# Weight loads issued in another place of GpSimd's queue, and another bias in the order of the last part

## The chip, the cores and the metric

The kernel runs on one core of one Trainium2 chip. The metric is the device time of an execution in microseconds, here the median of nine runs. A profile comes from one further execution; its times have their zero at the first instruction of the span.

## The reference

Two layers. The first is attention with a soft cap over 8 batches, 12 heads, 448 tokens and heads of 64: `softmax(cap * tanh(q k^T / 8 / cap)) v` with `cap = 30`. Its result, `x` of shape (8, 448, 768), goes into the second, a mixture of four attention experts with causal masks:

```
logits = x @ w_gate                      # 4 experts, the best 2 are kept per token
w = softmax over the 2 kept logits
for e in range(4):
    q, k, v = x @ wq[e], x @ wk[e], x @ wv[e]          # 768 -> 64 each
    a = softmax(causal(q k^T / 8))
    out += mask_e * w_e * (a @ v @ wo[e])              # 64 -> 768
```

## The kernel before

**Units of work.** The first layer goes by pairs of heads: 48 pairs, six for a batch. For each pair q, k and v are loaded in f32, cast to f16 (`a_cast`, on GpSimd from pair 2 on), q and k are transposed on TensorE (`a_tr`), the scores come in four fills of PSUM (`fill`, L470 to L484), ScalarE takes the tanh of each fill (L510) and then one exponential over the whole pair (L516). The product with v (`a_pv`, L544 and L550) is divided by the row sums and transposed into `xT`, the input of the second layer. Two PSUM buffers hold score fills, so that a fill waits for the tanh of the fill two before it.

When the six pairs of a batch stand in `xT`, the second layer of that batch is planned (`batch`, L1120): projections q and k for two groups of heads, `r` 0 and 1 (L724), values and gate logits in one product with `wvg` (L640; this tile holds the value weights of all four experts and the gate's), the scores and their exponential (L781), the product with the values (L808), and the output projections `wops` (L863) with their evacuation into `ob` and a store.

**Order.** The order of ScalarE's work is written out as a list `prog`: slot p (`("S", p)`), then the tanhs of pair p with the exponential of pair p - 1 and those of the second layer (`"X"`) between them. What TensorE and VectorE do between the fills is chosen while the program is built, by `Plan`: it keeps modelled times of the engines and, in `plan.done`, of each result, has a list of work with costs and due times, and always takes from what can start first the item with the earliest due time. A load of weights is such a result too: key `("w", ("q", r))`, `("w", ("k", r))`, `("w", "v")` or `("w", "o")`, with a time that is set when it is issued. Those times are read when `batch(0)` puts the projections of batch 0 on the list at slot 6. They change the order in which TensorE gets its instructions, not what an instruction waits for on the chip.

**Slots.** `slot(p)` (L1046) issues the loads of later pairs on SyncE, casts pair p + 4 on GpSimd, and issues weight loads on GpSimd's queue. GpSimd does its instructions in order, so that a weight load behind a cast leaves when the cast has had its data. There are 16 weight loads in the list `loads` (L961): q and k of expert 0, q and k of expert 1, four of `wvg`, q and k of experts 2 and 3, four of the output weights. Before the change each of the slots 0 to 7 issues two, behind its cast (L1064 to L1068), and gives them the time `plan.act + 26`, where `plan.act` is ScalarE's modelled time.

**The last part.** When the list is through, what is left of batch 6 and the second half of batch 7 (`last_batch`, L1250) is put into a `Graph` with costs, engines and PSUM banks. `solve` draws 4000 orders: each is built as a list schedule that takes, among what can start within a short time of the first, the operation of highest priority; priorities are the length of the longest path to the end plus a bias, changed at random by up to 3 us for some operations, and the order with the shortest modelled end is kept. The biases are set in L1273. BW is subtracted for the output projections and the stores of batch 6 (`c` in the code), so that -5 puts them forward by 5 us:

```
elif key[0] in ("wo", "st"):
    bias = BA * (key[1] == b and key[2] < 2) - BW * (key[1] == c)
```

Of the kernel before, what the change touches and what calls it, by code (L numbers as in the profile page):

```python
# [239 lines left out]
def kernel(  # L240
# [13 lines left out]
    nc = tc.nc  # L254
# [39 lines left out]
    def load(p, n=2):  # L294

        b, j = divmod(p, HP)
        h0, h1 = 2 * j, 2 * (j + n)
        qf = stage.tile([QP, 2 * n, QC * Dh], f32, name=f"qf_{p}", tag="qf")
        kf = stage.tile([128, 2 * n, KC * Dh], f32, name=f"kf_{p}", tag="kf")
        vf = stage.tile([128, 2 * n, KC * Dh], f32, name=f"vf_{p}", tag="vf")  # L300
        ktf = stage.tile([128, n, Dh], f32, name=f"ktf_{p}", tag="ktf")
        vtf = stage.tile([128, n, Dh], f32, name=f"vtf_{p}", tag="vtf")
        for i in range(n):
            h = slice(2 * i, 2 * i + 2)
            staged[p + i] = (qf[:, h], kf[:, h], vf[:, h], ktf[:, i], vtf[:, i])

        def rows(dst, src, c):
            return lambda eng: eng.dma_start(dst, src.rearrange("h (p c) d -> p h (c d)", c=c))

        def tails(dst, src, i):  # L310
            t = src[b, h0:h1, KM:S].rearrange("(j two) p d -> two p j d", two=2)
            return lambda eng: eng.dma_start(dst[64 * i : 64 * (i + 1)], t[i])

        return [
            rows(qf, q[b, h0:h1], QC), rows(kf, k[b, h0:h1, 0:KM], KC), tails(ktf, k, 0),
            tails(ktf, k, 1), rows(vf, v[b, h0:h1, 0:KM], KC), tails(vtf, v, 0), tails(vtf, v, 1),
        ]
# [6 lines left out]
    def ahead(p, n, since, more=4):  # L324

        new = range(p + n + more * (p > since), p + n + more * (p >= since) + 1)
        return [i for i in new if i < NP]
# [48 lines left out]
    def a_cast(p):  # L376
        if p >= NP:
            return
        eng = nc.vector if p < 2 else nc.gpsimd
        assert p < 8 or ("tr", p - 8) in plan.done  # L380
        assert p < 12 or ("pv", p - 12, 1) in plan.done
        qf, kf, vf, ktf, vtf = staged.pop(p)
        q16 = hd.tile([QP, QC, 2, Dh], f16, name=f"q16_{p}", tag="q16", bufs=8)
        k16 = hd.tile([128, KC, 2, Dh], f16, name=f"k16_{p}", tag="k16", bufs=8)
        eng.tensor_copy(q16, qf.rearrange("p h (c d) -> p c h d", c=QC))  # L385
        nc.gpsimd.tensor_copy(  # L386
            k16, kf.rearrange("p h (c d) -> p c h d", c=KC)
        )
        for g in range(2):
            r = slice(64 * g, 64 * (g + 1))  # L390
            eng.tensor_copy(ktz[p % 8][r, r], ktf[r, :])  # L391
        cast[p] = (q16, k16)
        vcast[p] = (vf, vtf)
        if p > 1:
            a_castv(p)
# [506 lines left out]
    plan = Plan()  # L902
# [35 lines left out]
    def b_const(i):  # L938
        if i == 0:
            nc.gpsimd.memset(ltm, 0.0)  # L940
            nc.gpsimd.affine_select(
                out=ltm, in_=ltm, compare_op=ALU.is_ge, fill=-60000.0, base=0,
                pattern=[[1, 128]], channel_multiplier=-1,
            )
        else:
            nc.vector.memset(vtL, 0.0)
            nc.vector.memset(vtL[64:128, :, Dh : Dh + 1], 1.0)
        nc.vector.memset(vtB[i], 0.0)
        nc.vector.memset(vtB[i][0:64, 0:E:2, Dh : Dh + 1], 1.0)
        nc.vector.memset(vtB[i][64:128, 1:E:2, Dh : Dh + 1], 1.0)  # L950
        for t in pB[2 * i : 2 * i + 2]:
            nc.vector.memset(t[:, 0:64], 0.0)
# [8 lines left out]
    loads = []  # L961
# [81 lines left out]
    for p in range(len(UNITS), NP + HP + 4):  # L1043
        nom.setdefault(("S", p), t)

    def slot(p):  # L1046

        plan.work[:] = [u for u in plan.work if u["key"][0] != "warm"]
        n = 9 if p < 3 else 6 if p < 7 else 3 if p < 13 else 0
        for i in range(n):  # L1050
            plan.done["from", p, i] = nom["S", p] + 7.0 + 5.6 * i / n
            plan.add(("warm", p, i), 0.22, 0.0, [("from", p, i)], 1.0e9, keep_warm)
        if p % 2 == 0:
            for i in ahead(p, LOAD, DEEP):
                if i % 2 == 0:
                    for f in load(i):
                        f(nc.sync)
        for i in ahead(p, CAST, DEEP + 2):
            a_cast(i)
            plan.done[("cast", i)] = max(  # L1060
                5.65 * i + 1.5 if i < 12 else 0.0,
                plan.act + 4.0 + 3.5 * (i - p - CAST) * (p == DEEP + 2),
            )
        for _ in range(2):  # L1064
            if loads:
                w, dst, src = loads.pop(0)
                nc.gpsimd.dma_start(dst, src)
                plan.done["w", w] = plan.act + 26.0  # L1068
        if p in (4, 5):
            b_const(p - 4)  # L1070
        for i in (1, 2) if p == 0 else ahead(p, TR, DEEP + 4, 4):
            plan.add(("tr", i), 0.43, 0.95, [("cast", i)], nom["S", i] - 3.0, a_tr, i)
        if 1 <= p < len(UNITS):
            u = UNITS[p - 1]
            es = [("E", u)]
            due = nom["S", p + 1] + 2.0
            if isinstance(u, tuple):
                i = "AB".index(u[1])
                u = u[0]
                plan.parts(("pv", u, i), 2, 0.47, 0.55, es, due, a_pv, u, i)  # L1080
                d = [("pv", u, i)]
                plan.add(("xt", u, "AB"[i]), 0.12, 0.27, d, due, a_xt_part, u, i)
            else:
                plan.parts(("pv", u, 0), 2, 0.47, 0.55, es, due, a_pv, u, 0)
                d = [("pv", u, 0)]
                plan.parts(("pv", u, 1), 2, 0.47, 0.55, d, due, a_pv, u, 1)
                plan.add(("xt", u), 0.22, 0.35, [("pv", u, 1)], due, a_xt, u)
        if p >= HP and p % HP == 0 and p < NP:
            batch(p // HP - 1)
        if p == NP - 1:  # L1090
            last_qk()
        if p == NP:
            last_vg()
# [6 lines left out]
    def last_qk():  # L1100
        for r in range(2):
            g = ("qk", "A", r)
            due = nom["X", B - 1, r, 0] - 2.0
            for j in range(NDC):
                d = [x_of(j, "A"), ("w", ("q", r)), ("w", ("k", r))] + [(*g, j - 1)] * (j > 0)
                plan.add(
                    (*g, j), 0.22, 0.66 * (j == NDC - 1), d, due, qk_mm, "A", r, j,
                    aux={0: "open", NDC - 1: "close"}.get(j), group=g,
                )
# [10 lines left out]
    def batch(b):  # L1120
        x = ("xt", HP * b + HP - 1)
        t0, t1 = nom["X", b, 0, 0], nom["X", b, 1, 0]
        for r, t in enumerate((t0, t1)):
            plan.parts(("q", b, r), 3, 1.13, 0.55, [x, ("w", ("q", r))], t - 4.0, b_qk, b, r, "q")
            plan.parts(("k", b, r), 3, 1.13, 0.55, [x, ("w", ("k", r))], t - 4.0, b_qk, b, r, "k")
        for n in range(4):
            d = [("v", b, n - 1)] if n else [x, ("w", "v")]
            plan.parts(("v", b, n), 2, 0.66, 0.6, d, t0 + 2.0 * n, b_v, b, n)
        plan.add(("g1", b), 0.0, 1.0, [("v", b, 3)], t1 + 1.0, b_gate, b, aux=None)
        plan.add(("g", b), 0.0, 0.8, [("g1", b), ("G", b)], t1 + 3.0, b_gate2, b, aux=None)  # L1130
        for e in range(E):
            due = t1 + 6.0 + 3.0 * e
            d = [("X", b, e // 2, 1), ("g", b)] + [("pvB", b, e - 1)] * (e % 2)
            plan.add(("pvB", b, e), 0.31, 0.7, d, due, b_pv, b, e)
            if e % 2:
                plan.add(("oT", b, e // 2), 0.22, 0.35, [("pvB", b, e)], due, b_ot, b, e // 2)
        for n in range(4):
            for f in range(2):
                i = 2 * n + f
                d = [("oT", b, 1), ("w", "o")] if i == 0 else [("wo", b, *divmod(i - 1, 2))]  # L1140
                due = t1 + 19.0 + 1.5 * i
                plan.add(("wo", b, n, f), 0.33, 0.5, d, due, b_wo, b, n, f)
# [107 lines left out]
    def last_batch():  # L1250


        p, b = NP - 1, B - 1
# [16 lines left out]
            dict(aux=[(0.0, t) for t in plan.aux], tail=[(0.0, t3)] * 4),  # L1270
        )

        BR, BA, BW, BX = 0.0, 0.0, -5.0, 0.0  # L1273

        BOTH = ("aux", "tail")

# [124 lines left out]
        n = S - CUT  # L1401
# [75 lines left out]
        done = {}  # L1477
# [126 lines left out]
    for pos, o in enumerate(prog, 1):  # L1604
# [22 lines left out]
        while nfill < len(reads) and nfill - 2 in ends and all(  # L1627
            plan.known(d) for d in fill_dep(reads[nfill])
        ):
            do_fill()  # L1630
    last_batch()
# [1 line left out]
_INS = ['q', 'k', 'v', 'cap', 'moe_w_gate', 'moe_wq', 'moe_wk', 'moe_wv', 'moe_wo']  # L1633
# [31 lines left out]
```

## Time and profile before

| | us |
|---|---|
| median of 9 runs | 324.34 |
| lowest and highest | 322.97, 327.56 |
| profiled execution, its own time | 322.86 |
| its span, first to last instruction | 321.1 |
| ScalarE busy | 306.5 |
| TensorE busy (matmul) | 284.9 |
| GpSimd busy | 157.0 |
| share of the 16 DMA engines: SyncE's queue, GpSimd's queue | 52.0%, 6.8% |

In the rows of slices each digit is a fortieth of the span, 8 us, in tenths of busy time. A row of a timeline has start, length, engine, line and operation, the result and its inputs, and in brackets the idle time ahead of it and what ended that. A row of waits has who waited for what, the sum, the number and the longest. The chain is the work that ended last, followed back from the end.

### The profile page before, as it was taken

Reading aid. Unit: us, or ns where it says so; the run is one execution under the profiler, and the core shown is the slowest. Engines: PE = TensorE matmul, PEld = TensorE weight load, DVE = VectorE, ACT = ScalarE, POOL = GpSimd, SP = SyncE. Lnnn points to the kernel's source line nnn. Section 1 sums busy time; section 2 is a strip of 40 time slices with the busy share of each in tenths; the row PEclk is TensorE's granted clock in tenths of the full one; section 3 lists DMA queues with packets and bytes.
Section 4 is the critical chain, followed back from the end, with each engine's and each line's share of the span. In section 5 each row is a group of like instructions: output and inputs, shape, how many; then the busy total and the mean of one; then the engine's idle time right before and its main releaser. Section 6 shows DMA issues by size and latency. Waiting matters only on the chain.

```text
span 321.1 us, 9088 instructions
## 1 busy us (share of the span) xinstructions
PE 284.9 (89%) x3439; PEld 179.5 (56%) x3439; DVE 216.2 (67%) x760; ACT 306.5 (95%) x311; POOL 157.0 (49%) x480
## 2 busy tenths in 40 slices
PE   8887878997999889997799899997999878999993
PEld 2454444664565656565556565655655654557761
DVE  4444544587586877678867876767856975578673
ACT  3999997999999999999999999999999999999973
POOL 4639999956706299874904386082905200220200
PEclk9999999999999999999999979999899999999998
DMA  8679999998025999577082934586012102020045
GB/s 166 176 190 257 226 227 230 241 228 160 1 100 145 254 259 268 160 203 170 2 224 110 281 80 143 161 229 157 3 52 98 27 2 99 2 77 2 3 171 174
DMA packets 65404, 46.22 MB, mean 144 GB/s; under 512 B 26000, under 2 KB 61968, under 8 KB 65360
## 3 DMA queue, kind: packets, MB, share of 16 engines
q1 hardware_dynamic: 54064, 43.28, 52.0%
q0 software_dynamic: 10512, 1.58, 6.8%
q10 hardware_dynamic: 784, 0.77, 0.9%
q8 instruction: 27, 0.44, 0.6%
q14 instruction: 17, 0.14, 0.1%
HBM read 36.19 MB, written 11.01 MB: 147 GB/s over the span
## 4 chain that ended last, share of the span: by engine, by line
ACT 66%; PE 15%; issue 7%; DMA 5%; POOL 4%; DVE 1%; SPq 0%; DVEq 0%; POOLq 0%
ACT y L510 32%; ACT p L516 25%; ACT pBs L781 8%; DMA wvg<-in_moe_wv_dram 4%; PE vps L640 2%; PE wops L863 2%; DMA vf<-in_v_dram 1%; PE pv L550 1%; PE dummy L898 1%; PE qkA L1166 1%; PE pv L544 1%; PE pvB L808 1%; PE qkB L1166 1%; POOL v16s L399 1%; POOL q L385 1%
## 5 line engine op out<-in xcount | busy, mean ns | idle before, releaser
L510 ACT ACTIVATE y<-s 128x896 f16<-128x896 f32 (+1 forms) x176 | 138.2, 928 | 2.3 <-PE s L476 2.2
L516 ACT ACTIVATE p<-y 128x3136 f16<-128x3136 f16 x44 | 128.3, 2915 | 0.1
L789 POOL TENSOR_SCALAR_AFFINE_SELECT pBs<-pBs 128x128 f16<-128x128 f16 (+1 forms) x112 | 28.2, 278 | 106.1 <-ACT pBs L781 104.9
L550 PE MATMUL pv<-v16s,p 128*128 128x65 f16 x1056 | 56.3, 194 | 0.0
L480 PE MATMUL s<-qt,kt 64*128 64x448 f16 x264 | 47.5, 362 | 9.5 <-ACT y L510 7.4
L550 PEld LDWEIGHTS <-p 128*128 128x128 f16 x1056 | 47.6, 98 | 3.9 <-issue 0.4
L544 PE MATMUL pv<-vtzs,p 128*128 128x130 f16 x176 | 39.6, 225 | 8.3 <-ACT p L516 6.3
L559 DVE RECIPROCAL rc<-pv 128x4 f32<-128x4 f32 x96 | 17.2, 179 | 38.2 <-PE pv L550 36.9
L563 DVE TENSOR_TENSOR xk<-pv,rc 128x256 f16<-128x256 f32 x96 | 40.7, 424 | 3.3
L370 DVE COPY ob<-wops 128x384 f32<-128x384 f32 (+1 forms) x54 | 29.9, 553 | 7.0 <-PE wops L863 6.7
L480 PEld LDWEIGHTS <-kt 64*128 64x128 f16 x264 | 16.0, 93 | 29.5 <-issue 22.9
L544 PEld LDWEIGHTS <-p 128*128 128x128 f16 x176 | 17.1, 97 | 27.1 <-ACT p L516 14.7
L385 POOL CAST q<-qf 112x512 f16<-112x512 f32 x46 | 28.1, 611 | 7.7 <-DMA qf<-in_q_dram 5.9
L640 PE MATMUL vps<-wvg,xT 128*128 128x260 f16 (+1 forms) x192 | 30.3, 275 | 1.5 <-DMA wvg<-in_moe_wv_dram 1.5
L781 ACT ACTIVATE pBs<-sB 128x960 f16<-128x960 f32 (+1 forms) x28 | 30.7, 1111 | 0.0
L863 PE MATMUL wops<-wo,oT 128*128 128x384 f16 x128 | 30.6, 327 | 0.0
L399 POOL CAST v16s<-vf 128x384 f16<-128x384 f32 x48 | 24.3, 507 | 5.0 <-DMA vf<-in_v_dram 2.2
L386 POOL CAST k<-kf 128x384 f16<-128x384 f32 x48 | 24.3, 506 | 3.8 <-DMA kf<-in_k_dram 3.8
L370 DVE COPY xT<-xtp 128x448 f16<-128x448 f16 (+2 forms) x50 | 18.6, 374 | 8.9 <-PE xtp L585 7.7
L404 POOL CAST vtzs<-vtf 64x64 f16<-64x64 f32 x96 | 22.6, 235 | 3.4 <-DMA vtf<-in_v_dram 0.5
L898 PE MATMUL dummy<-warm 128*128 128x512 f16 x67 | 21.8, 414 | 1.3 <-DVE warm L330 1.3
L391 POOL CAST ktzs<-ktf 64x64 f16<-64x64 f32 x92 | 21.3, 232 | 2.8
(180 smaller groups left out, 528.6 us busy)
## 6 DMA issues: line engine op xcount, KB each, us to landing
qf<-in_q_dram SPq DMA_DIRECT2D x22, 448.0 KB, 5.8
out_dram<-ob SPq DMA_DIRECT2D x23, 384.0 KB, 2.3
kf<-in_k_dram SPq DMA_DIRECT2D x22, 384.0 KB, 6.5
vf<-in_v_dram SPq DMA_DIRECT2D x22, 384.0 KB, 6.1
out_dram<-ob SPq DMA_DIRECT2D x8, 192.0 KB, 2.8
ktf<-in_k_dram SPq DMA_DIRECT2D x44, 32.0 KB, 5.8
vtf<-in_v_dram SPq DMA_DIRECT2D x44, 32.0 KB, 4.9
kf<-in_k_dram SPq DMA_DIRECT2D x4, 192.0 KB, 3.3
```

The lines of the kernel that those rows point to most:

```text
L370: (nc.scalar.copy if act else nc.vector.tensor_copy)(dst, src)
L385: eng.tensor_copy(q16, qf.rearrange("p h (c d) -> p c h d", c=QC))
L480: nc.tensor.matmul(sc[:, g, 0:S], kt[r, 128 * i : 128 * (i + 1)], qt[r, :], start=True, stop=True,)
L510: nc.scalar.activation(dst, src, AF.Tanh, scale=isc / capf)
L516: nc.scalar.activation(pt[:, 0:n], y.pop(u)[:, 0:n], AF.Exp, scale=capf)
L544: nc.tensor.matmul(pv[:, n, :, :], prob(p, w, 0, 0), vtz[p % 12], start=(n == 0), stop=False, skip_group_check=True,)
L550: nc.tensor.matmul(pv[:, n, g, :], prob(p, w, j, g), v16[p % 12][:, g, j - 1, :], start=False, stop=(j == KC), skip_group_check=True,)
L563: nc.vector.tensor_tensor(xt[p][:, 2 * i : 2 * i + 2, :, :], pv[:, :, :, 0:Dh], rc.broadcast_to((128, 2, 2, Dh)), ALU.mult,)
L640: nc.tensor.matmul(ps, xT[b][:, j, w : w + 128], wvg[:, j, 0 : ps.shape[1]], start=(j == 0 and first), stop=(j == NDC - 1), skip_group_che ...
L781: nc.scalar.activation(pb[:, o0 : o0 + n], st[b].pop(("sc", r, g))[:, 0:n], AF.Exp, scale=isc)
L789: nc.gpsimd.affine_select(out=blk, in_=blk, compare_op=ALU.is_ge, fill=0.0, base=0, pattern=[[1, n]], channel_multiplier=-1,)
L863: nc.tensor.matmul(ps, st[b]["oT", r][:, w : w + 128], wo2[r][:, f * (D // 2) : (f + 1) * (D // 2)], start=(r == 0), stop=(r == 1),)
```

## The change

The weight loads get a function of their own, with the time that the planner is to reckon with. In slot 0 four are issued ahead of the cast of pair 4 (the q and k weights of experts 0 and 1, time 30.0) and none behind it. Slots 1 to 6 issue two each behind their cast as before, so that each later load is issued one slot earlier: `wvg` in slots 1 and 2, not 2 and 3. Their time is `plan.act + 20`, or `37.0 + 4.2 * p` where that is later. In the last part BW goes from -5 to 0, and the output projections and stores of batch 6 have no bias.

```diff
+    def load_weights(n, done):
+        for _ in range(min(n, len(loads))):
+            w, dst, src = loads.pop(0)
+            nc.gpsimd.dma_start(dst, src)
+            plan.done["w", w] = done
+
     def slot(p):
...
+        if p == 0:
+            load_weights(4, 30.0)
         for i in ahead(p, CAST, DEEP + 2):
             a_cast(i)
...
-        for _ in range(2):
-            if loads:
-                w, dst, src = loads.pop(0)
-                nc.gpsimd.dma_start(dst, src)
-                plan.done["w", w] = plan.act + 26.0
+        if p:
+            load_weights(2, max(plan.act + 20.0, 37.0 + 4.2 * p))
...
-        BR, BA, BW, BX = 0.0, 0.0, -5.0, 0.0
+        BR, BA, BW, BX = 0.0, 0.0, 0.0, 0.0
```

## The prediction

> **What bounds the kernel now.** I read the busy times first, then the slices, then the waits, then the timelines of the stretches that the diff touches.
>
> ```profile
> PE 284.9 (89%) x3439; PEld 179.5 (56%) x3439; DVE 216.2 (67%) x760; ACT 306.5 (95%) x311; POOL 157.0 (49%) x480
> ACT  3999997999999999999999999999999999999973
> DMA  8679999998025999577082934586012102020045
> ```
>
> ScalarE is the bound: 306.5 of 321.1 us, and every slice is a 9 but the first, the seventh (48 to 56 us) and the last two. Only what starves ScalarE in between, or lengthens the tail, moves the end. The list of waits for 0 to 70 us names the seventh slice, the timelines of ScalarE and TensorE show it:
>
> ```profile
> ACT y L510 <- PE s L476: 2.2, 2, 1.7
> PE vps L640 <- DMA wvg<-in_moe_wv_dram: 1.5, 1, 1.5
> ```
>
> ```profile
> 48.27 0.54 PE L724 MATMUL qps<-xT,wq 128*128 128x448 f16 x2
> 50.30 0.51 PE L640 MATMUL vps<-wvg,xT 128*128 128x260 f16 x3 [1.49 <-DMA wvg<-in_moe_wv_dram]
> 50.65 0.35 PE L476 MATMUL s<-qt,kt 128*128 128x448 f16 x1
> ```
>
> ```profile
> 51.03 0.54 ACT L510 ACTIVATE y<-s 128x448 f16<-128x448 f32 x1 [1.75 <-PE s L476]
> ```
>
> TensorE is in order. The first value projection of batch 0 waits 1.49 us for the last `wvg` load; behind it stands a score fill (L476), and for that ScalarE waits 1.75 us. From there on ScalarE runs without a gap worth a name until 304.1 us, so what is won at 51 us reaches the end.
>
> **Part 1: the weight loads.** The loads leave GpSimd's queue between its casts, and that queue is in order (its timeline, columns start, length, instruction, idle before):
>
> ```profile
> 17.00 0.53 POOL L404 CAST vtzs<-vtf 64x64 f16<-64x64 f32 x2
> 21.67 0.61 POOL L385 CAST q<-qf 112x512 f16<-112x512 f32 x1 [4.14 <-DMA qf<-in_q_dram]
> 22.88 0.51 POOL L386 CAST k<-kf 128x384 f16<-128x384 f32 x1 [0.60 <-DMA kf<-in_k_dram]
> ...
> 25.45 0.84 POOL L1067 DMA_DIRECT2D wq<-in_moe_wq_dram  x1
> ...
> 33.86 1.64 POOL L1067 DMA_DIRECT2D wvg<-in_moe_wv_dram  x2
> ...
> 38.06 1.64 POOL L1067 DMA_DIRECT2D wvg<-in_moe_wv_dram  x2
> ```
>
> *What moves.* Four issues of 0.83 us, 3.3 us, go into the idle 4.14 us ahead of pair 4's cast: 17.53 + 3.3 = 20.85, before 21.67. The issuing itself costs nothing; the cover is 0.8 us, and without it each late microsecond would fall on pair 4's cast, behind which only casts and weights are queued. No work is added, no wait either (the tiles are fresh), and the queue of SyncE is not passed. Pair 5's cast (2.5 us, its data came with pair 4's) then starts at 25.45, `wvg` 0 and 1 leave at 28.0 to 29.6, pair 6's cast follows to 32.1, and the last `wvg` issue is at 32.9, where it was 38.88. It took 11.4 us to land (38.88 to 50.30). With the same 11.4 it lands at 44.3; if pair 4's values hold the queue 1.5 us longer, at 45.8. It is wanted at 48.81 (50.30 less 1.49). Margin 3 us: **the wait goes, minus 1.49 us.**
>
> *What is late next.* The fill at 50.65 comes at 49.16. ScalarE had been free since 49.28 (51.03 less 1.75), so 0.26 of its 1.75 us stays. After that, the second q and k weights: they would leave near 38 and 42 to 44 us and land by 57.5 (the slowest `wk` took 13.6 us), and are first used at 61.99. The planner would now allow 53.8 (37.0 + 4.2 x 4) where it allowed about 58; if it used that at once, TensorE would wait up to 3.5 us. But their due times stand behind those of the values and of the first heads, and before they were used 4 us after they were allowed. I take nothing. The output weights leave 4 us earlier and are wanted a batch later: nothing.
>
> *What it costs.* The four transfers now share the DMA engines with pair 4's loads. Who waits for these: the transposes of pair 4 on TensorE, with the probabilities and the next score fill behind them.
>
> ```profile
> 23.91 0.23 PE L419 MATMUL tps<-ident,ktzs 128*128 128x128 f16 x1 [0.18 <-POOL ktzs L391]
> ...
> 24.68 0.23 PE L544 MATMUL pv<-vtzs,p 128*128 128x130 f16 x1 [0.37 <-ACT p L516]
> ...
> 25.48 0.36 PE L480 MATMUL s<-qt,kt 64*128 64x448 f16 x2
> ```
>
> There is no slack in front (0.18 us is already waited), but behind: 0.37 us of waiting for ScalarE at 24.68, about 0.2 ahead of 25.48, and the fill ends at 25.84 where ScalarE wants it at 26.12 (24.48 plus two halves of 0.82). Together 0.85 us; a delay d of pair 4's keys costs ScalarE d less 0.85. How large is d? No row shows four weights at that place. Nearest is the load for pair 8, issued together with the first two weights, against that of pair 4 (DMA issues, last number us to landing):
>
> ```profile
> kf<-in_k_dram SPq DMA_DIRECT2D x1, 384.0 KB, 6.6
> ```
>
> ```profile
> kf<-in_k_dram SPq DMA_DIRECT2D x1, 384.0 KB, 7.8
> ```
>
> That is 1.2 us, or 2.2 against the 5.6 of pair 6: a cost of 0.35 to 1.35. Against the change speaks the Trainium skill, "DMA: Bandwidth & Descriptors", section "Queues, rings and completion order": each DMA engine takes turns between the rows that have work, packet by packet, so the small weight packets are not kept behind the big loads. A weight load is 768 rows; at 33 ns for a packet of that queue (6.8% of 16 x 321.1 us over 10512) it is 1.6 us of all 16 engines, four are 6.4. By the rule pair 4's keys, 3.4 us from landing when the weights begin to move (about 19.5), would take twice as long: d = 3.4, cost 2.55. The rows say less, as the engines are not full there: 110 GB/s from 20.5 to 21.5, where they reach 350. And the keys are issued 1.3 us ahead of the first weight, those of pair 8 1.4 behind it. I take the lower row and less, d = 0.9 to 1.0: **plus 0.1** (0 to 2.55; no gain, as nothing there becomes earlier).
>
> **Part 2: the bias of the last part.** BW from -5 to 0 takes 5 us of rank from batch 6's output projections and stores in the search for an order. No instruction is added or removed. Seven of the eight projections lie in that part, between 302.7 and 308.7 us: 7 x 0.33 = 2.3 us of TensorE, which is dense there. The chain of the end then has a hole:
>
> ```profile
> 311.06 0.12 PE vps L640
> ...
> 311.21 0.44 DVE vtL L370
> ...
> 311.67 0.38 ACT vall L370
> ...
> 312.10 0.52 PE pvLB L1519 x12
> ```
>
> TensorE does nothing from 311.2 to 312.1, 0.9 us. Projections pushed back could fill it: two of 0.33 fit, and what was behind them comes earlier by as much; at most minus 0.9. On the other side, all seven behind the last chain: their evacuations, 0.48 us on ScalarE and 0.55 on VectorE, shared by both, are 7 x 0.5 / 2 = 1.8 us, and their stores, of about 2.6 us to landing, follow: plus 1.8, and 1.3 more (half a landing, an estimate from that row) if the stores meet the last ones. The search takes the shortest modelled order of 4000 with either bias, so ends near the present one are likelier than either bound. I take **minus 0.3**.
>
> **Sum.** -1.49 + 0.1 - 0.3 = -1.7 us. The profiled execution took 322.86 us (span 321.1 and 1.8 around it): 321.2. The median of the runs shown is 324.34, 1.5 above it; less 1.7 it is 322.6. About 0.5% (1.6 us) is what a measurement of this kernel can tell from no change, and the forecast stands just beyond that.
>
> **The rivals.** *The gain is only part of it, within 0.5% (323.6).* ScalarE's saving at 51 us is met by a small loss: pair 4 late by 1.5 us (cost 0.65), or a last part that is 0.5 longer. For it: the sum passes the bound by 0.1 only, and 0.26 us of the stall stays anyway. That the change does nothing is hard to see: the wait is there, and the load leaves 6 us earlier.
>
> *Pair 4 pays (325.4).* The weights take the place of the wait they remove: the engines share by turns, d is 3.4, ScalarE stalls 2.55 us near 26 us, net 2.55 - 1.49 = +1.1. It decides from d = 2.35 (0.85 + 1.49). For it: 6.4 us of transfers in front of keys that are already waited for. Against: rows of 1.2 and 2.2, and engines half idle at that time.
>
> *The last part comes out worse (326).* The projections pile up behind the last chain: +1.8 and stores that collide, +1.3; 3.1 less 1.4 is net +1.7. It decides from 1.4 lost in the tail. For it: evacuations are what ScalarE and VectorE do last. Against: the search counts them, and the DMA engines are nearly idle from 312 to 314.
>
> **How the numbers follow.** Forecast 322.6 at 0.47, own range 321.2 to 322.9; partial gain 0.28; pair 4 pays 0.13; worse last part 0.12. Of the last two about 0.16 lie beyond +0.5%, the rest within: faster 0.47, same 0.37, slower 0.16. The range reaches from 321.2 (all of the hole filled and all of the stall gone, -1.75 - 0.9 = -2.65, and 0.5 for the measurement; some 0.07 below) to 326.2 (one of the two costs at its upper bound and a part of the other; some 0.1 above).
>
> **What would show it.** Right: in the profile after, four weight issues stand between 17.5 and 21 us ahead of pair 4's cast, the last `wvg` issue near 33 to 35, no wait of L640 for `wvg`, ScalarE's gap near 50 us at most 0.3, the seventh slice a 9. Wrong: pair 4's key cast later than 24, a gap of ScalarE between 25 and 28, a new wait of L724 for `wq` or `wk`, or more than 17 us from ScalarE's last exponential of the first part (304.1) to the end of the span (321.1). The forecast fails most easily by the last part, which no row prices.

## The result and the profile after

| | before | after |
|---|---|---|
| median | 325.67 (52 runs) | 322.44 (17 runs) |
| lowest and highest | 322.33, 330.49 | 321.37, 323.85 |
| ratio to before | 1 | 0.9914, 95% interval 0.9892 to 0.9937 |
| profiled execution, its span | 322.86, 321.1 | 322.17, 320.4 |

All times are in microseconds. The kernel became faster by 0.86%, some 2.8 us; the forecast was 1.7. The ratio leaves out slow executions, those over 1.5% above the fastest of their kernel, and the medians do not, so they lie 3.2 us apart. The nine runs shown before had a median of 324.34; over all runs of the kernel before it is 325.67. What stands out is the spread: the runs of the kernel before lie over 8 us, those of the changed one over 2.5.

The two profiles alone would say 0.7 us. ScalarE's row of slices has no dent left:

```profile
PE 282.8 (88%) x3438; PEld 178.3 (56%) x3438; DVE 216.1 (67%) x760; ACT 306.4 (96%) x311; POOL 157.4 (49%) x480
ACT  3999999999999999999999999999999999999882
```

TensorE's timeline of the changed kernel around batch 0's first projections, where 1.49 us of waiting for `wvg` stood before:

```profile
48.53 0.54 PE L724 MATMUL qps<-xT,wq 128*128 128x448 f16 x2
48.91 0.50 PE L640 MATMUL vps<-wvg,xT 128*128 128x260 f16 x3
49.25 0.35 PE L476 MATMUL s<-qt,kt 128*128 128x448 f16 x1
```

The projection follows at once, the score fill comes 1.4 us earlier, and ScalarE has no gap over 0.15 us from 7.3 us to the end of the first layer at 302.9 us. GpSimd's timeline shows where the loads went:

```profile
20.11 0.85 POOL L1049 DMA_DIRECT2D wk<-in_moe_wk_dram  x1
21.29 0.61 POOL L385 CAST q<-qf 112x512 f16<-112x512 f32 x1 [0.33 <-DMA qf<-in_q_dram]
22.61 0.51 POOL L386 CAST k<-kf 128x384 f16<-128x384 f32 x1 [0.70 <-DMA kf<-in_k_dram]
...
34.02 1.65 POOL L1049 DMA_DIRECT2D wvg<-in_moe_wv_dram  x2
```

Four issues end at 20.96, pair 4's casts start where they did (21.67 and 22.88 before), the idle 4.14 us ahead of them are 0.33. The last `wvg` issue is at 34.8 (before 38.88); the load takes 9.6 us to land (before 11.4).

At the other end time is given back. Counted from the last exponential of the first layer (it starts at 302.90 before, 301.54 after), the last evacuation ends after 14.1 us before and 13.5 after, but the span ends after 18.2 and 18.9. The stores have become slower. The issues from 310 us on show it, first in the changed kernel, then in one with the weights part alone (E3 below). The columns are the count, the size and the time to landing in us. The kernel before has the same 2.6 us for its two of 384 KB.

```profile
out_dram<-ob SPq DMA_DIRECT2D x4, 384.0 KB, 3.7
out_dram<-ob ACTq DMA_DIRECT2D x2, 192.0 KB, 4.4
```

```profile
out_dram<-ob SPq DMA_DIRECT2D x2, 384.0 KB, 2.6
out_dram<-ob ACTq DMA_DIRECT2D x1, 192.0 KB, 3.0
```

With BW = 0 two more stores of 384 KB, batch 6's, stand in front of the last ones.

### The profile page after: what moved, and what is told of

Read it like the earlier page. It is cut to its first block, busy times and chain, and to the rows that moved or that the text cites. A ratio compares the mean times of both kernels' runs of the same rounds, so it can differ in the third digit from the quotient of the medians.

```text
span 320.4 us, 9085 instructions
## 1 busy us (share of the span) xinstructions
PE 282.8 (88%) x3438; PEld 178.3 (56%) x3438; DVE 216.1 (67%) x760; ACT 306.4 (96%) x311; POOL 157.4 (49%) x480
## 4 chain that ended last, share of the span: by engine, by line
ACT 78%; PE 12%; issue 6%; DMA 1%; DVE 1%; POOL 0%; POOLq 0%
ACT y L510 37%; ACT p L516 30%; ACT pBs L781 8%; PE wops L863 2%; PE vps L640 2%; DMA qf<-in_q_dram 1%; PE pv L550 1%; PE qkA L1171 1%; ACT pB L516 1%; PE pv L544 1%; PE kps L724 1%; ACT yB L510 1%; ACT pBs L1244 1%; PE sB L762 0%; PE qps L724 0%
## 5 line engine op out<-in xcount | busy, mean ns | idle before, releaser
L510 ACT ACTIVATE y<-s 128x896 f16<-128x896 f32 (+1 forms) x176 | 139.7, 959 | 0.5 <-PE s L476 0.5
L516 ACT ACTIVATE p<-y 128x3136 f16<-128x3136 f16 x44 | 129.7, 2948 | 0.1
L550 PE MATMUL pv<-v16s,p 128*128 128x65 f16 x1056 | 55.6, 193 | 0.0
L550 PEld LDWEIGHTS <-p 128*128 128x128 f16 x1056 | 46.9, 97 | 3.4
L544 PEld LDWEIGHTS <-p 128*128 128x128 f16 x176 | 17.0, 97 | 30.7 <-ACT p L516 17.7
L863 PE MATMUL wops<-wo,oT 128*128 128x384 f16 x128 | 29.9, 327 | 0.3 <-ACT oT L370 0.3
L431 DVE COPY qt<-tps 128x384 f16<-128x384 f16 x48 | 16.8, 351 | 8.9 <-PE tps L421 8.3
```

What stands on the lines that cost most here:

```text
L510: nc.scalar.activation(dst, src, AF.Tanh, scale=isc / capf)
L516: nc.scalar.activation(pt[:, 0:n], y.pop(u)[:, 0:n], AF.Exp, scale=capf)
L544: nc.tensor.matmul(pv[:, n, :, :], prob(p, w, 0, 0), vtz[p % 12], start=(n == 0), stop=False, skip_group_check=True,)
L550: nc.tensor.matmul(pv[:, n, g, :], prob(p, w, j, g), v16[p % 12][:, g, j - 1, :], start=False, stop=(j == KC), skip_group_check=True,)
L863: nc.tensor.matmul(ps, st[b]["oT", r][:, w : w + 128], wo2[r][:, f * (D // 2) : (f + 1) * (D // 2)], start=(r == 0), stop=(r == 1),)
```

## The experiments

Each ratio is that to the kernel before, run on the same chip in the same job, with its 95% interval. "Tail" is the time in the profile from the start of the exponential of gate A (`eexpA`), which follows the last exponential of the first layer, to the end of the span: 16.97 us before, 17.63 after.

**E1, the issue order alone.** The loads leave as in the change; the planner reckons with the old times, so that no other engine has another order. BW is -5.

```diff
+    names = [x[0] for x in loads]
...
-            plan.done["w", w] = done
...
-            load_weights(2, max(plan.act + 20.0, 37.0 + 4.2 * p))
+            load_weights(2, 0.0)
+        for _ in range(2):
+            if names:
+                plan.done["w", names.pop(0)] = plan.act + 26.0
...
-        BR, BA, BW, BX = 0.0, 0.0, 0.0, 0.0
+        BR, BA, BW, BX = 0.0, 0.0, -5.0, 0.0
```

> GpSimd issues its weight loads as in the changed kernel; the planner reckons with the old times, so that TensorE, VectorE, ScalarE and SyncE have the order of before, and the bias stays at -5. Theory A (the wait for wvg is the whole gain; other executions of the kernel before wait longer than the profiled one, so its median hides a longer stall): ratio 0.991 to 0.993, ScalarE's gap near 50 us under 0.3. Rival B (the new order of TensorE around batch 0 makes the gain): ratio 1.000. Rival C (the last part makes what goes beyond the 1.6 us of the profiled gap): ratio 0.995.

Measured: 0.9899 (0.9845 to 0.9952), median 321.3. ScalarE has no gap near 50 us, tail 17.0. TensorE goes from the projection to the fill at once:

```profile
48.80 0.50 PE L640 MATMUL vps<-wvg,xT 128*128 128x260 f16 x3
49.14 0.35 PE L476 MATMUL s<-qt,kt 128*128 128x448 f16 x1
```

The place in GpSimd's queue makes the gain, not TensorE's order. The gain is 3.3 us, with an interval from 1.6 to 5.1 us: it lies above the 1.49 us of the profile, but how far above is loosely known.

**E2, the bias alone.**

```diff
-        BR, BA, BW, BX = 0.0, 0.0, -5.0, 0.0
+        BR, BA, BW, BX = 0.0, 0.0, 0.0, 0.0
```

> Kernel before with BW = 0 alone. Theory A with the tail as the two profiles have it (last evacuation 0.6 us earlier against the last exponential, stores 1.3 later): ratio 1.000 to 1.003. Rival C: ratio 0.996. The wait for wvg and ScalarE's gap near 51 us stay as before.

Measured: 1.0039 (1.0009 to 1.0069), tail 18.56. The bias part costs about 1.3 us (0.3 to 2.3); the two profiles had said 0.7.

**E3, the weights part alone** (the change with BW = -5).

> The changed kernel with BW back at -5. Theory A: ratio 0.990 to 0.992, at or a little under the changed kernel (up to 0.6 us, as the tail of before is that much shorter). Rival C: ratio 0.995, over the changed kernel by 1.3 us.

Measured: 0.9878 (0.9832 to 0.9924), median 321.13, tail 16.95. With 1.0039 for the bias this gives 0.992, and the whole change has 0.991: within the intervals the parts add up.

**E4, the kernel before once more,** for a profile of another execution.

> The kernel before once more, for a second profile and for the noise of a ratio: 1.000. Theory A: where this profiled execution takes longer than 322.9 us, ScalarE's gap near 51 us is longer than 1.75 by about as much (near 4 us at 325 us). Rival C, and a spread that comes from elsewhere: the gap is 1.5 to 2 us again whatever the time.

Measured: 1.0002 (0.9970 to 1.0034). The profiled execution took 325.9 us, and shows what the first one did not have. TensorE's timeline, then ScalarE's:

```profile
51.61 0.56 PE L640 MATMUL vps<-wvg,xT 128*128 128x260 f16 x3 [2.75 <-DMA wvg<-in_moe_wv_dram]
51.97 0.58 PE L476 MATMUL s<-qt,kt 128*128 128x448 f16 x1
52.34 0.95 PE L724 MATMUL qps<-xT,wq 128*128 128x448 f16 x2
```

```profile
52.58 0.54 ACT L510 ACTIVATE y<-s 128x448 f16<-128x448 f32 x1 [3.25 <-PE s L476]
58.26 0.92 ACT L510 ACTIVATE y<-s 128x896 f16<-128x896 f32 x1 [0.82 <-PE s L480]
```

The wait is 2.75 us and not 1.49, and the matmuls behind it are slower: two of L724 take 0.95 us, where they took 0.54. ScalarE starves a second time, 0.82 us at 58 us. The table of stretches of the same profile has the reason. Its columns are the stretch, its length, the busy time of TensorE with the number of instructions, the granted clock, the DMA share (above 1 where packets overlap in time) and GB/s:

```profile
50.00:52.00 2.00, 0.39 (x4) 0.98 1.55 257
52.00:54.00 2.00, 2.00 (x12) 0.50 1.49 221
54.00:56.00 2.00, 2.00 (x20) 0.66 1.41 216
56.00:58.00 2.00, 2.00 (x26) 1.00 1.39 218
```

The granted clock falls to half, for 3.4 us. In E2's profile, with the loads of before, the wait is 2.69 us, the clock is at half for 6.8 us, and ScalarE loses 3.45 and then 1.80 us.

**E5, TensorE kept busy through the wait.** Sixteen idle matmuls stand ahead of the projection that waits; nothing else is changed.

```diff
         ps = s["vps", n]
+        if (b, n, i) == (0, 0, 0):
+            for _ in range(16):
+                nc.tensor.matmul(
+                    ps, warm[:, 0:128], warm[:, 0 : E * Dh + E], start=True, stop=True,
+                    skip_group_check=True,
+                )
         b_v_mm(b, n, ps, 3 * i, 3 * i + 3, True)
```

> The kernel before, its weight loads and its bias untouched; 16 idle matmuls of 260 columns (1.8 us) into the bank of batch 0's first value projection stand ahead of that projection, so that TensorE works through most of the wait for wvg. Theory A2 (a long wait also drops TensorE's granted clock to half for some 4 to 6 us, and this starves ScalarE a second time): the granted clock stays at 1.00 behind the wait, ScalarE's second gap (0.8 and 1.8 us in the two profiles with a long wait) is gone, the first stays; ratio 0.995 to 0.998. Rival (only the landing of wvg counts, the clock is a bystander): ratio 1.000, or up to 1.002 as the idle matmuls outlast a short wait by 0.3 us.

Measured: 0.9975 (0.9948 to 1.0003). In the profile the clock stays at 1.00 and ScalarE has one gap there, not two:

```profile
51.42 0.49 PE L640 MATMUL vps<-wvg,xT 128*128 128x260 f16 x3 [0.77 <-DMA wvg<-in_moe_wv_dram]
```

```profile
52.14 0.54 ACT L510 ACTIVATE y<-s 128x448 f16<-128x448 f32 x1 [2.78 <-PE s L476]
```

The direction is the expected one, but the interval touches 1. That the clock costs something over the wait is seen in the traces of E2 and E4; how much it is worth in the median (about 0.8 us here) is not settled. Nor does one profile at 1.00 show that the idle matmuls held the clock: in E10 below it stayed at 1.00 behind a longer wait without them.

**E6, eight loads ahead of pair 4's cast.** BW is -5, and the planner gets the times of the change, by a function of its own (`plan_weights`).

```diff
...
-            load_weights(4, 30.0)
+            load_weights(8, 0.0)
+            plan_weights(4, 30.0)
...
```

> Weights part alone (BW = -5) with eight loads ahead of pair 4's cast where the change has four; planner's times and so the order of the other engines as in the weights part alone. Theory (the four fit the idle 4.1 us of GpSimd, behind it each microsecond falls on pair 4 beyond a slack of 0.85 us): eight issues take 6.6 us, pair 4's q cast comes near 24.3 us and not 21.3, ScalarE stalls near 26 us by 1.7 to 2.6 us; no wait for wvg; ratio to before 0.993 to 0.997, against 0.988 with four. If the transfers as such cost nothing and pair 4 has more slack than I read: 0.988.

Measured: 0.9943 (0.9915 to 0.9971). Pair 4's q cast comes at 24.47, TensorE's transposes of it wait, and ScalarE loses 0.94 us at 27 us. The mechanism of the rival "pair 4 pays" exists; four loads stay clear of it, by the profile after. The price is lower than I expected: pair 4's last transposes come 2.25 us later than in the changed kernel (26.06 against 23.81), ScalarE loses 0.94, so that the slack is 1.3 us in this profile and not 0.85.

**E7, four loads in slot 0, but behind pair 4's cast.** BW is -5.

```diff
-        if p == 0:
-            load_weights(4, 30.0)
         for i in ahead(p, CAST, DEEP + 2):
...
-        if p:
+        if p == 0:
+            load_weights(4, 30.0)
+        else:
             load_weights(2, max(plan.act + 20.0, 37.0 + 4.2 * p))
...
```

> Weights part alone (BW = -5), but slot 0 issues its four loads behind pair 4's cast, not ahead of it; orders of the other engines the same. If the gain comes from each load leaving one slot earlier: last wvg issue near 36.5 us, landing near 47, no wait or a small one, ratio 0.988 to 0.991. If the place ahead of pair 4's cast is what counts: wvg comes too late in part of the executions, ratio 0.993 to 0.997.

Measured: 1.0037 (1.0008 to 1.0066), slower than before, and against both expectations. My own theory falls here: the last `wvg` load left at 36.1, 2.8 us earlier than before, and landed at 50.7, no earlier than before. It took 14.6 us. TensorE waits for it, and a second time for the q weights of experts 2 and 3, which the planner now takes to be there at 53.8 us:

```profile
50.75 0.51 PE L640 MATMUL vps<-wvg,xT 128*128 128x260 f16 x3 [1.91 <-DMA wvg<-in_moe_wv_dram]
60.12 0.90 PE L724 MATMUL qps<-xT,wq 128*128 128x448 f16 x2 [3.08 <-DMA wq<-in_moe_wq_dram]
```

So the loads do not land a fixed time after they leave. From the issues of each load and its time to landing, the landings (us) are as follows, each cell in order of issue:

| load | before | E7 | after |
|---|---|---|---|
| q, k, q, k | 30.6, 34.0, 38.2, 41.3 | 32.4, 33.4, 35.6, 39.8 | 23.1, 23.8, 26.5, 28.8 |
| wvg 0 to 3 | 43.6, 46.0, 48.9, 50.3 | 42.9, 44.9, 47.9, 50.7 | 36.9, 37.9, 40.9, 44.5 |

Before and in E7 one load lands every 1 to 4 us, 2.6 to 2.8 on average, however early it left: the queue of the weight loads is backed up. In the changed kernel the first four have landed by 28.8 us, before the first `wvg` leaves at 29.8, and `wvg` finds no weight load ahead of it. What holds the queue up is the question of E9.

**E8, the change without batch 6's stores** (those rows of the output are not written).

```diff
     def b_store(b, n, fs=(0, 1), act=False):
+        if b == B - 2:
+            return
```

> The changed kernel (weights and BW = 0) without the stores of batch 6, whose rows of the output are not written; everything else is kept. If the bias part costs its time because batch 6's stores pile up with the last ones: landings of the last stores fall from 4.0 to about 2.7 us, the end comes 1.3 to 1.8 us earlier, from the last exponential (gate A) to the end 16 us, ratio 0.986 to 0.988. If the evacuations and not the stores are what costs: 17.3 us or more, ratio 0.990 to 0.992.

Measured: 0.9877 (0.9816 to 0.9937), tail 16.25 where the changed kernel has 17.63. The last stores land in 2.1 to 2.8 us:

```profile
out_dram<-ob SPq DMA_DIRECT2D x2, 384.0 KB, 2.5
out_dram<-ob ACTq DMA_DIRECT2D x2, 192.0 KB, 2.4
```

By the profiles, what the bias costs is the stores of batch 6 in front of the last ones; the ratio alone is too loose to say so (four runs). In this profile TensorE waits 0.69 us for `wq` of the second heads, and ScalarE loses 0.57 us.

**E9, two staging buffers and not four, in the kernel before.** Weight loads, planner, order and bias are as before; SyncE's loads no longer run ahead of the casts.

```diff
-    stage = ctx.enter_context(tc.tile_pool(name="stage", bufs=4))
+    stage = ctx.enter_context(tc.tile_pool(name="stage", bufs=2))
```

> The kernel before with two staging buffers for the loads of q, k and v where it has four; the order of every engine is the same, SyncE's loads of pairs 8 to 13 just have to wait for earlier casts and do not run ahead from 26 us on. Theory D (the weight loads land late because their queue moves slowly while SyncE's loads fill the DMA engines; the change wins because its first four leave before that): wvg lands in 8 us or less, no wait for it or one under 0.5 us, ratio 0.990 to 0.995 if the casts are not starved. Rival (the weight queue takes 2.5 to 3 us for a load by itself): landings near 11 us and the wait as before, ratio 1.000 or above.

Measured: 0.9861 (0.9813 to 0.9909), median 321.18. The `wvg` loads take 6.8 to 9.1 us to land where they took 9.8 to 11.4, the last is there at 47.6, no engine waits for it, and ScalarE runs without a gap over 0.15 us from 7 us to the end of the first layer:

```profile
48.62 0.50 PE L640 MATMUL vps<-wvg,xT 128*128 128x260 f16 x3
48.95 0.35 PE L476 MATMUL s<-qt,kt 128*128 128x448 f16 x1
```

The weight queue was slow because SyncE's loads filled the DMA engines; held back, they let it pass, at the place where it always was. The landings were expected in 8 us or less; the last took 9.1.

**E10, the planner's new times alone,** loads issued as before, BW = -5.

> Planner's times as in the change, loads issued where the kernel before issues them, BW = -5. If the gain were in the planner's order: ratio 0.990 to 0.995. By my theory the wait for wvg stays and the earlier projections of the second heads (planned from 53.8 us) run into wq and wk, which land near 58 to 61: further stalls of ScalarE of 3 us or more near 60 us, ratio 1.005 to 1.015.

Measured: 1.0065 (1.0037 to 1.0093). The planner's times without the earlier loads are a loss: a wait of 3.46 us for `wvg`, and one of 0.84 for `wq`, smaller than I expected. The granted clock stayed at 1.00 behind both.

```profile
52.61 0.51 PE L640 MATMUL vps<-wvg,xT 128*128 128x260 f16 x3 [3.46 <-DMA wvg<-in_moe_wv_dram]
```

**E11, the weights part without batch 6's stores** (not written).

> Weights part alone (BW = -5) without the stores of batch 6, whose rows of the output are not written. If with BW = -5 those stores end before the last ones begin, nothing is gained: from the last exponential (gate A) to the end 16.9 us as with them, ratio 0.987 to 0.989. If the stores load the end with either bias: 15.6 us, ratio 0.984.

Measured: 0.9889 (0.9843 to 0.9935), tail 17.2. With BW = -5 these stores cost nothing that shows (E3 has 0.9878 and 16.95): the counterpart of E8.

**E12, the weights part with BW = -10.**

```diff
-        BR, BA, BW, BX = 0.0, 0.0, 0.0, 0.0
+        BR, BA, BW, BX = 0.0, 0.0, -10.0, 0.0
```

> Weights part with BW = -10, batch 6 put forward by 10 us and not by 5. If more priority goes on helping: from the last exponential (gate A) to the end under 16.9 us, ratio 0.985 to 0.987. By my theory the stores are already out of the way at -5, and what remains is another order of about the same length: 0.987 to 0.990.

Measured: 0.9827 (0.9793 to 0.9862), median 320.66, the fastest of all and clear of the changed kernel's interval. The order moved the exponential of gate A behind two evacuations, so that the tail cannot be compared by it. From the start of the last exponential of the first layer (301.62) to the end it is 17.7 us, where E3 has 18.2; the spans, 319.3 and 319.2, are the same. Whether -10 is better than -5 is open, as the intervals overlap. That -10 is better than 0 with these weight loads is clear of both intervals; for -5 the intervals of E3 and of the changed kernel overlap, and it rests on E2 and on the tails of E3, E8 and E11.

## Why the prediction was right or wrong

**The wait for `wvg` goes: right, and it is the gain.** E1 has it with every other engine's order unchanged. The fill at 49.2, the seventh slice a 9 and the idle GpSimd time filled are as predicted.

**Minus 1.49: too small, the term that was mis-sized.** The weights part is worth 4.0 us (0.9878 of 326.2; by the interval 2.5 to 5.5). I took the wait from one execution, which at 322.86 stood near the fast end of its kernel's runs, and set the result against a median 1.5 us above it without asking where those 1.5 us came from. E4 and E2 show the same wait at 2.7 us, with a drop of the clock and a second gap behind it, 4.2 and 5.4 us of ScalarE in all. The granted clocks of the runs fit this. On the chip of E3 the two executions of the kernel before at 1.00 took 322.61 and 323.11 us, and E3's three at 1.00 took 320.95 to 321.08: some 1.8 us apart, about the profile's gap of 1.75. So some 2 of the 4 us lie in executions whose clock had fallen. Whether the fall costs them, or only comes with the longer waits, is not settled: E5 gives the clock about 0.8 us, not clear of nothing, and E10's execution at 1.00 took 325.79. The spread of the runs shown, 323 to 327.6, was a hint that I did not use.

**"With the same 11.4 it lands at 44.3": the right time for a wrong reason.** It landed at 44.5, but after 9.6 us from an issue 1.9 us later than I reckoned. Time to landing is no constant here: it is the time in a queue that is backed up behind SyncE's loads (E7 14.6 us, E9 9.1). By my reasoning E7 would have won.

**Pair 4 pays plus 0.1: nothing.** Its key cast came at 22.61 and not later; only its values came 0.8 us later (25.30 against 24.52). The rule of taking turns, which I weighed at d = 3.4, did not show on the keys. What showed was the other queue: the weight loads wait for SyncE's (E9), for up to 11.4 us to landing before, against 1.6 us of transfer for one by the estimate of the prediction. Whether they do so by turns, no run here shows. E6 shows the price that I named for a late pair 4, 0.94 us.

**The second q and k weights, "I take nothing": nearly wrong.** The planner did use the earlier time. Their first product stands at 55.03 in the profile after, not at 60.5 (61.99 less 1.49), and the q weights land at 52.9. In E8 and E12 the wait is 0.7 and 0.5 us, in E7 3.08. The margin is 2.1 us where I had reckoned 3 and more.

**The last part, minus 0.3: wrong side.** E2 says plus 1.3. The step that failed is "ends near the present one are likelier than either bound". The hole was also smaller than I read it. The chain shows what released what, not all that TensorE did; its own timeline before has 0.49 us of idle time and not 0.9:

```profile
311.10 0.34 PE L1448 MATMUL sLB<-qkB,qkA 64*128 64x192 f16 x4
311.38 0.24 PE L1519 MATMUL pvLB<-vall,pBs 128*128 128x65 f16 x2
312.10 0.37 PE L1519 MATMUL pvLB<-vall,pBs 128*128 128x65 f16 x7 [0.49 <-ACT vall L370]
```

It was filled, and the last evacuation ends 0.6 us sooner; but the stores went with the projections, and I had kept them for the bad case only. One of my signs of being wrong came: over 17 us from the exponential of gate A to the end, 17.63. The rival "the last part comes out worse" had the mechanism right, though it alone could not make the kernel slower: it needed more than 1.4 us, and the gain beside it was 4.0 and not 1.5.

**The sum.** -4.0 + 0 + 1.3 is -2.7, measured -2.8. The forecast of 322.6 met 322.44 because two errors, 2.5 us too little and 1.6 too much, worked against each other, and because the median I started from was 1.3 us lower than that of all runs. That the number met is luck; the direction and the mechanism of part 1 are not.

## What to carry to other kernels

A wait for a DMA in one profile is one draw: where runs spread, take a second profile before pricing it, and ask what the wait does to the engine behind it. A load's time to landing belongs to its queue and to what else the DMA engines hold (E7, E9), so ask when the engines are free and not only how early the load leaves; holding back a prefetch that runs too far ahead did as much here as moving the late loads (E9). Work that is pushed back to fill a hole takes its stores along: look at the last landing, not at the last instruction of an engine.

## What the runs showed of the hardware

**The clock.** TensorE's granted clock fell to half behind waits of 2.69 us (E2), 2.75 (E4) and 3.08 (E7), and stayed there for 6.8, 3.4 and 3.4 us. It did not behind 1.49 (before), 1.91 (E7) and 3.46 us (E10). So the length of the wait alone does not decide. The first profile of the kernel before has two more drops of 3.4 us, at 186.3 and 223.9 us, with no idle time of TensorE over 1.5 us ahead of them; ScalarE has no gap over 0.15 us there. In one profile the drops begin a whole number of 3.41 us apart: 37.5 us, or 11 of them, between these two, and 139.9 us, or 41, between two of E2. Laid on this grid, the windows of 3.41 us look as follows, first one before and the drop behind it, then the two that share E10's wait, with no drop (columns as in E4):

```profile
182.93:186.34 3.41, 1.72 (x33) 1.00 1.05 272
186.34:189.75 3.41, 3.17 (x39) 0.50 0.21 53
```

```profile
47.42:50.83 3.41, 1.73 (x26) 1.00 1.60 242
50.83:54.24 3.41, 1.63 (x15) 1.00 1.38 205
```

TensorE was busy for 0.33 us (E7), 0.66 (E4), 1.33 (E2), 1.72 and 1.86 us (before) of the window ahead of a drop. The wait of E10 was long, but it lay across a border, and neither window had less than 1.63 us of work. So it counts how much of a wait falls into one window; with about half a window of work, both outcomes occur. The Trainium skill, "TensorE: Matmul & The Clock Gate", section "Part 1: The HAM clock gate (the "warmup" mystery)", says that the clock is set by windows of 3.4 us that run freely, and halves after an idle one. The grid and the lengths at half clock agree; that the window must be idle does not, as the measured ones had up to 1.86 us of work. Where a wait falls on the grid is a matter of chance in each execution, and this is one likely source of the spread of the kernel before.

**Stores.** From 310 us on the changed kernel moves 1.46 MB up to 316 us, E3 0.91; landings of the last stores of 192 KB on ScalarE's queue are 4.4 us and 3.0.
